# Two head pairs' queries and keys transposed on TensorE instead of by DMA, with a new written order of the whole kernel

## The chip, the cores and the metric

The kernel runs on one core of a Trainium2 chip. Its time is the device time of that core in microseconds (us), the median of several runs; the profile is that of one further execution. The engines are TensorE (PE, matrix products; PEld are its weight loads), VectorE (DVE), ScalarE (ACT), GpSimd (POOL) and SyncE (SP, which here only issues DMAs). Each engine works through its own instructions in order and waits where another engine or a DMA has not yet delivered.

## The reference, cut to what matters

A block-sparse attention is followed by a two-layer MLP with squared ReLU.

```python
B, H, S, D = 4, 8, 768, 64          # batches, heads, sequence, head size
scores = q @ k.T / sqrt(D)          # per batch and head, 768 x 768
mask = near the diagonal (blocks of 32, one to each side)
       | first or last block row or column
       | 3 sampled blocks of keys for each block of queries
attn = softmax(where(mask, scores, -1e9)) @ v
x = attn as 3072 tokens x 512
h = x @ w_in                        # 512 -> 2048
g = maximum(h, 0) ** 2
y = g @ w_out                       # 2048 -> 512
```

## The kernel before

**Tiling.** Two heads make a head pair (2 x 64 = 128 partitions), so there are 16 pairs, numbered u = 0 to 15; pair u belongs to batch u // 4. Queries come in three pieces of 256 columns. The scores are computed transposed (keys on the partitions), exponentiated by ACT (`exps`, line 360, and `s_exps`, line 643), masked, multiplied with the values (`values_full`, line 398, and `s_values`, line 673), normalized, transposed back (`x_transp`), and go as tiles of 256 tokens into the MLP: `hidden` (x with w_in), `relu` (lines 727 and 729), `square` (lines 738 and 740), and `out` matmuls with `out_copy` and `store`. Batches 0 and 1 compute all scores and mask them; batches 2 and 3 compute only the chosen blocks, with gathered keys and values. Nearly all matmuls are issued by one helper, `pair` (line 203), so the profile shows them as L203; copies and casts by `copy` (line 121 on ACT, 123 on DVE and POOL).

**PSUM.** Four cells of 1024 fp32 columns, called X, take the results of PE; a task names the cell that it uses.

**Queries and keys.** They arrive in fp32, are cast to bf16 (`cast_qk`, into a buffer `qc`) and must be transposed so that the head dimension is on the partitions (`QKT`). `prepare` builds the tasks for this. For the first four pairs, the transposes run on PE (`transp`, line 305) into an X cell, from which `evac` copies them to `QKT`. For pairs 4 and up a DMA transposes from `qc` to `QKT` directly (`transp_dma`, line 312), issued on SP's queue. `old_s` are the scores of the pair that used the same place of `QKT` before.

**The mask of the first two batches.** `mask_rows` (line 258) computes rows of the mask on PE, in two pieces (columns 0 to 256 and 256 to 768), and `mask_rows_evac` copies them to the bf16 tile `R2` (shown as R). In the first scores the mask is added on PE itself (matmuls `X<-R,oh`); the later masks are tiles made by `mask_tile` and `mask_evac` and are multiplied on DVE.

**Weights.** `w_load` (lines 328 and 331) loads w_in (0 to 3) and w_out (4 to 7) in eight parts of 512 KB on POOL's queue, starting once the last values of batch 0 have landed. `loads_gate` (line 338) puts two tiny DMAs into SP's queue that read from parts 6 and 7, so that the loads of batch 1 behind them (`load`, lines 149 and 151) start only when these two parts are there.

**The order.** The work is a list of tasks, and one long string, `PROGRAM`, says which task is issued when and on which engine. A word such as `P260/3` means: task 260 on PE, with cell 3 of PSUM; V, A, G and S stand for DVE, ACT, POOL and SP. `run_program` goes through the string once and issues the instructions; on each engine they then run in that order. Which engine does a cast, a square or a copy is chosen by the letter too.

```python
for word in PROGRAM.split():
    i, _, spot = word[1:].partition("/")
    t = tasks[int(i)]
```

Of the kernel before, what the change touches and what calls it, by code (L numbers as in the profile page):

```python
# [25 lines left out]
def kernel(  # L26
# [127 lines left out]
    KEYS, ALL = (slice(0, CP), slice(CP, NCH)), slice(0, NCH)  # L154
# [41 lines left out]
    X = [ps_x.tile([P, 1024], F32, name=f"X{i}").rearrange("p (h c) -> p h c", h=2) for i in range(NX)]  # L196
# [606 lines left out]
    def T_(f, *args, **kw):  # L803
        return Task((lambda e: f(*args, e)), **kw)
# [10 lines left out]

    def prepare(u):
        ev[u] = {}
        n_old = u - NPB
        old_s = sc_of[n_old] if n_old >= 0 else []
        old_v = va_of[n_old] if n_old >= 0 else []  # L820
        if u >= HP:
            g = gate[GATES[min(u - HP, len(GATES) - 1)]]
            for w in range(3):
                raw_of[u, w] = Buf(RAWS[w])
            ld_t = [T_(load, u, w, get=[raw_of[u, w]], deps=[g] + raw_claims[-1:]) for w in range(3)]
            at = [ld_t[2]]
            for w in (1, 0):
                qc = Buf("qc")
                c = T_(cast_qk, u, w, ALL, get=[qc], put=[raw_of[u, w]], deps=[ld_t[w]])
                buf_of["qc", u, w, 0] = qc  # L830
                cq[u, w] = [c]
                x = T_(transp_dma, u, w, deps=[c] + old_s, put=[qc])
                ev[u].update({(w, n): x for n in range(NCH)})
        else:
            at = []
            own = range(3 if u < 2 else 1 if u == 2 else 0)
            for w in own:
                raw_of[u, w] = Buf(RAWS[w])
# [116 lines left out]
    t = T_(table_load, deps=[])  # L955
# [3 lines left out]
    hb = Buf("X")  # L959
    t = T_(table_spread, hb, deps=[tb["slots"]], get=[hb], put=tmp)  # L960
# [3 lines left out]
    for us in [range(b * HP, (b + 1) * HP) for b in range(B)]:  # L964
        for u in us:
            prepare(u)
        mine = [a for a in order if a[0] in us]
        if us[0] < HP:
            for c0, c1 in MASKED:
                for n in range(0, NCH, 2):  # L970
                    mb = Buf("X")
                    t = T_(mask_tile, n, c0, c1, mb, get=[mb], deps=mr)
                    x = T_(mask_evac, n, c0, c1, deps=[t, mk_claims[[m_[0] for m_ in MASKED].index(c0)]], put=[mb])
                    for c in range(c0, c1, P):
                        mk[n, c] = mk[n + 1, c] = x
        if us[0] >= SB * HP:
            b = us[0] // HP
            vw = T_(v_store, b, deps=sum((cv[u] for u in us), []))
            for v in range(len(VISITS)):
                visit(b, v, vw, [a for a in mine if a[1] == v * P])  # L980
            continue
        for a in mine:
            attend(a, us[0] < HP and a[1] == 0)

    sq_of, gbuf = {}, {}
    for T in TILES:
# [3 lines left out]
        for f in range(0, NF, n_u):  # L990
            hb, ht, rb, gb = Buf("X"), Buf("H"), Buf("r"), Buf("g")
# [16 lines left out]
        for i, y in enumerate(ys):  # L1008
# [44 lines left out]
```

## Time and profile before

| | |
|---|---|
| median of 3 runs | 258.85 us (258.25 to 259.73) |
| the profiled execution | 258.04 us |
| its span in the trace | 256.3 us |
| PE busy | 244.4 us, 95% of the span, 5265 matmuls |
| ACT busy | 183.4 us, 72% |
| DVE busy | 173.0 us, 67% |
| POOL busy | 100.3 us, 39% |
| moved by DMA | 47.08 MB, 184 GB/s on average |

A profile has a page for the whole span (busy times, the chain of work that ended last, groups of instructions by line), and the trace behind it gives the single instructions. In a timeline row the columns are the start in us, the duration in us, the engine, the line of the code, the operation and its tiles as out<-in with their shapes, and in brackets the time that the engine had been idle before and what ended that. In a row of stretches there is for each engine the busy time and the number of its instructions, then PE's granted clock as a share of full speed, the busy share of the DMA engines and GB/s. In a row of groups, the busy sum and the mean duration in ns stand behind the first bar, the idle time before and its releasers behind the second. A row of the chain has start, length and what the chain was in.

### The profile page before, as it was taken

Reading aid. Unit: us, or ns where it says so; the run is one execution under the profiler, and the core shown is the slowest. Engines: PE = TensorE matmul, PEld = TensorE weight load, DVE = VectorE, ACT = ScalarE, POOL = GpSimd, SP = SyncE. Lnnn points to the kernel's source line nnn. Section 1 sums busy time; section 2 is a strip of 40 time slices with the busy share of each in tenths; the row PEclk is TensorE's granted clock in tenths of the full one; section 3 lists DMA queues with packets and bytes.
Section 4 is the critical chain, followed back from the end, with each engine's and each line's share of the span. In section 5 each row is a group of like instructions: output and inputs, shape, how many; then the busy total and the mean of one; then the engine's idle time right before and its main releaser. Section 6 shows DMA issues by size and latency. Waiting matters only on the chain.

```text
span 256.3 us, 12057 instructions
## 1 busy us (share of the span) xinstructions
PE 244.4 (95%) x5265; PEld 183.4 (72%) x5265; DVE 173.0 (67%) x411; ACT 183.4 (72%) x217; POOL 100.3 (39%) x178
## 2 busy tenths in 40 slices
PE   7988999989999999998999999999999999999994
PEld 5667779759975579975866766857774677666674
DVE  7678997789998999869939647656636725730301
ACT  3799999978999799946695975585965186623640
POOL 3264228002407006198558424174448620413100
PEclk9999999999999999999999999999999999999999
DMA  6999998999799997999589899996484922034122
GB/s 191 364 246 205 206 208 128 252 255 241 190 262 232 207 239 141 313 217 201 191 232 207 226 170 212 251 190 186 115 203 98 195 47 50 16 102 145 46 84 84
DMA packets 64692, 47.08 MB, mean 184 GB/s; under 512 B 31567, under 2 KB 60624, under 8 KB 64640
## 3 DMA queue, kind: packets, MB, share of 16 engines
q1 hardware_dynamic: 58512, 37.82, 63.0%
q0 software_dynamic: 5440, 8.05, 16.9%
q8 instruction: 41, 0.67, 1.2%
q10 hardware_dynamic: 688, 0.46, 0.6%
q14 instruction: 11, 0.09, 0.2%
HBM read 35.51 MB, written 7.91 MB: 169 GB/s over the span
## 4 chain that ended last, share of the span: by engine, by line
PE 68%; DMA 16%; DVE 4%; POOL 4%; SPq 3%; issue 2%; ACT 1%; DVEq 0%; POOLq 0%
PE X L203 63%; DMA w_out_sb<-in_moe_w_out_dram 5%; PE X L673 5%; DMA ys<-in_v_dram 3%; DMA QKT<-qc 3%; DMA ks<-in_k_dram 2%; DMA qs<-in_q_dram 2%; DMA VG<-rows 1%; SPq L556 1%; POOL qc L123 1%; POOL w_in_sb L328 1%; SPq L560 1%; POOL VB L123 1%; ACT pT L643 1%; POOL g L740 1%
## 5 line engine op out<-in xcount | busy, mean ns | idle before, releaser
L203 PE MATMUL X<-xT,w_in_sb 64*128 64x256 bf16 x1536 | 100.0, 269 | 0.6 <-issue 0.4
L203 PE MATMUL X<-w_out_sb,g 64*128 64x512 bf16 (+3 forms) x960 | 95.4, 334 | 0.2
L203 PEld LDWEIGHTS <-w_in_sb 64*128 64x128 bf16 x1536 | 74.9, 94 | 12.3 <-issue 1.2
L360 ACT ACTIVATE pT<-X 128x1024 bf16<-128x1024 f32 x72 | 70.4, 1031 | 8.5 <-PE X L203 8.0
L203 PEld LDWEIGHTS <-g 64*128 64x128 bf16 x960 | 40.2, 94 | 26.7 <-issue 0.6
L643 ACT ACTIVATE pT<-X 128x768 bf16<-128x768 f32 (+1 forms) x56 | 41.5, 765 | 24.2 <-PE X L203 20.9
L740 POOL TENSOR_TENSOR g<-r 128x1024 bf16<-128x1024 f32 (+1 forms) x20 | 31.6, 1587 | 67.3 <-ACT r L727 50.0
L727 ACT ACTIVATE r<-X 128x1024 f32<-128x1024 f32 x28 | 29.8, 1070 | 20.6 <-PE X L203 16.9
L729 DVE TENSOR_SCALAR r<-X 128x1024 f32<-128x1024 f32 x20 | 24.5, 1224 | 26.9 <-POOL g L740 10.2
L367 DVE TENSOR_TENSOR pT<-pT,VG 128x1024 bf16<-128x1024 bf16 x60 | 41.5, 724 | 0.7 <-ACT pT L360 0.7
L738 ACT ACTIVATE g<-r 128x1024 bf16<-128x1024 f32 (+1 forms) x40 | 35.3, 901 | 2.7 <-DVE r L729 2.5
L203 PE MATMUL X<-QKT 64*128 64x256 bf16 (+1 forms) x384 | 32.9, 255 | 3.8 <-DMA QKT<-qc 1.2
L650 DVE TENSOR_TENSOR pT<-pT,MKS 128x768 bf16<-128x768 bf16 (+1 forms) x48 | 28.6, 629 | 8.7 <-ACT pT L643 8.6
L203 PEld LDWEIGHTS <-QKT 64*128 64x128 bf16 x384 | 16.9, 97 | 10.5 <-issue 4.4
L597 POOL DMA_INDIRECT VG<-rows,idx x19 | 21.2, 1118 | 4.6 <-issue 2.3
L203 PEld LDWEIGHTS <-pT 64*128 64x128 bf16 x768 | 16.1, 94 | 2.3 <-issue 0.3
L203 PE MATMUL X<-VB,pT 64*128 64x65 bf16 x768 | 17.4, 190 | 0.2 <-issue 0.2
L203 PEld LDWEIGHTS <-KG 64*128 64x128 bf16 x528 | 13.7, 95 | 5.0 <-issue 0.7
L203 PE MATMUL X<-QKT,KG 64*128 64x64 bf16 x528 | 15.3, 190 | 0.3 <-issue 0.2
L673 PEld LDWEIGHTS <-pT 128*64 128x64 bf16 x624 | 11.9, 111 | 5.0 <-issue 3.3
L679 DVE RECIPROCAL ss<-X 128x8 f32<-128x8 f32 x12 | 2.5, 206 | 18.8 <-PE X L673 16.8
L121 ACT COPY ys<-X 128x1024 f32<-128x1024 f32 (+1 forms) x10 | 9.7, 970 | 6.5 <-PE X L203 4.2
(107 smaller groups left out, 211.8 us busy)
## 6 DMA issues: line engine op xcount, KB each, us to landing
vs<-in_v_dram SPq DMA_DIRECT2D x14, 384.0 KB
ks<-in_k_dram SPq DMA_DIRECT2D x13, 384.0 KB
qs<-in_q_dram SPq DMA_DIRECT2D x12, 384.0 KB
out_dram<-ys SPq DMA_DIRECT2D x9, 512.0 KB
VG<-rows SPq DMA_DIRECT2D x20, 132.0 KB
w_in_sb<-in_moe_w_in_dram POOLq DMA_DIRECT2D x4, 512.0 KB, 8.8
w_out_sb<-in_moe_w_out_dram POOLq DMA_DIRECT2D x4, 512.0 KB, 9.5
rows<-VB SPq DMA_DIRECT2D x2, 792.0 KB
```

What stands on the lines that cost most here:

```text
L121: A.copy(out=out, in_=in_)
L203: last = nc.tensor.matmul(out(r ^ crossed), lhsT(r ^ crossed, rows), rhs(r ^ crossed, rows), skip_group_check=True, **kw)
L360: A.activation(out=pT[:, :, 0:n], in_=stile.pop(a)[:, :, 0:n], func=AF.Exp, scale=scale)
L367: V.tensor_tensor(out=pT, in0=pT, in1=m[:, None].broadcast_to([P, 2, len(cs), w]), op=AOP.mult)
L597: G.indirect_dma_start(out=to[0:RS * HB], out_offset=None, in_=pairs, in_offset=bass.IndirectOffsetOnAxis(ap=idx[0:RS * HB, g - 1:g], axis=0))
L643: A.activation(out=pT[:, :, 0:n], in_=stile.pop((u, v, gs))[:, :, 0:n], func=AF.Exp, scale=scale)
L650: V.tensor_tensor(out=pT, in0=pT, in1=m[:, None].broadcast_to([P, 2, n]), op=AOP.mult)
L673: nc.tensor.matmul(po[i * D:(i + 1) * D, h, a * VW:(a + 1) * VW], pts[g][:, h, c * D:(c + 1) * D], val, start=a == 0 and c == 0, stop=c == ...
L727: A.activation(out=to, in_=src, func=AF.Relu)
L729: V.tensor_scalar(out=to, in0=src, scalar1=0.0, scalar2=None, op0=AOP.max)
L738: A.activation(out=g, in_=r, func=AF.Square)
L740: (G if e == "POOL" else V).tensor_mul(out=g, in0=r, in1=r)
```

## The change

For pairs 4 and 5, the first two pairs of the second batch, queries and keys are transposed on PE into an X cell and copied to `QKT`, as for the first four pairs, in place of the DMA transpose: 48 transposes and four copies for four DMAs. The other pairs keep the DMA. Behind that, the string `PROGRAM` is new as a whole; the numbers of the tasks behind pair 4 shift by up to four.

```diff
+    BY_PE = (4,5)
+
     def prepare(u):
         ...
                 c = T_(cast_qk, u, w, ALL, get=[qc], put=[raw_of[u, w]], deps=[ld_t[w]])
                 buf_of["qc", u, w, 0] = qc
                 cq[u, w] = [c]
-                x = T_(transp_dma, u, w, deps=[c] + old_s, put=[qc])
+                if u in BY_PE:
+                    hb = Buf("X")
+                    t = T_(transp, u, w, ALL, hb, deps=[c], get=[hb], put=[qc])
+                    x = T_(evac, u, w, ALL, deps=[t] + old_s, put=[hb])
+                else:
+                    x = T_(transp_dma, u, w, deps=[c] + old_s, put=[qc])
                 ev[u].update({(w, n): x for n in range(NCH)})
...
-    PROGRAM = """A29 G35 P4/3 V32 P30/0 P12/2 P14/3 P9/1 P5/1 V31 P33/1 V111 P36/3 P0/2 A37 V1 V34 P102/2 ...
+    PROGRAM = """
+        S21 P2/0 S18 P0/3 A29 G35 P4/1 V1 V3 V32 P30/3 P12/2 P14/1 P9/2 P5/1 V31 P33/2 V111 P36/1 A37 V34 P102/0 V209 V46 P47/3 P106/2
...
```

What the new order moves, by engine:

- The start: the two `mask_rows` (P2 and P0) stand first on PE, and their copies (V1, V3) first on DVE, ahead of the cast of the second half of pair 0's keys (V32). Before, P0 stood behind the first transposes and P2 behind the scores of pair 1.
- The load of the table of sampled blocks (S21) stands first in SP's queue; POOL works out the table's places ahead of the weight loads.
- The weight loads on POOL's queue come in the order 1, 2, 7, 0, 6, 3, 4, 5 (before: 1, 2, 0, 3, 7, 6, 4, 5). POOL's casts of the values of pair 1 (G52) and pair 3 (G73) stand behind three and seven of them (before: behind two and three).
- Behind the gate SP issues the loads of keys 5, queries 4, queries 5, keys 4, values 4, queries 6. The casts are on POOL (queries 4, queries 5), DVE (keys 4) and ACT (keys 5), and the copies of the transposes on DVE (pair 4) and ACT (pair 5).
- All eight output parts of the first MLP tile stand ahead of the first scores of pair 4 on PE (before: four of them).
- Squares: ACT 24 (before 40), POOL 18 (20), DVE 18 (0). ReLUs: ACT 32 (28), DVE 16 (20). Casts of queries and keys: ACT 5 (2), POOL 22 (14), DVE 10 (21). Casts of values: ACT 2 (0), POOL 9 (10), DVE 5 (6). Output copies: ACT 7 (11), DVE 8 (4).
- The last piece of the output is 256 columns wide (before: 128).

More of the change, by code (lines that the diff above doesn't have):

```diff
@@ new lines @@
+    PROGRAM = """
+        S21 P2/0 S18 P0/3 A29 G35 P4/1 V1 V3 V32 P30/3 P12/2 P14/1 P9/2 P5/1 V31 P33/2 V111 P36/1 A37 V34 P102/0 V209 V46 P47/3 P106/2
+        A103 V48 P104/1 V43 A107 P44/3 G57 P7/0 V45 A105 P58/0 V54 P113/3 V59 P55/1 A114 P117/0 G41 V56 V67 A118 P115/1 P108/0 A116 V64
+        P127/3 V109 P10/2 P65/1 A128 P123/2 V66 A124 P68/1 P125/3 G22 G75 V69 V63 P92/1 P110 A126 P133/2 G76 G81 G38 G49 V112 A134 P39/0
+        P137/3 G52 S83 S19 S28 S20 S42 V40 V93 P88/0 A60 A138 V155 V89 P84/2 P119/1 G74 V70 V85 P61/3 P86/0 P135/2 V62 V120 G80 G77 G78
+        G73 A87 A136 P129/3 P121 V130 V122 P176/0 P131 P170/1 P139/2 A177 A171 V132 V140 P50/0 P71/3 P146/1 P141 V72 V142 V51 A147
+        P149/3 V172 A150 P173/2 V148 P785/0 A174 P786 V178 P189/1 P787 A190 V175 P90/3 P15/2 P96/2 P788 V91 P143/1 P8/3 A97 P183/2 V151
+        A789 P94/3 P179/0 V95 A184 G79 G791 P16/3 P186/2 P11/3 P778/3 V180 P779 A144 A790 V145 V191 P181 P157/1 P780 V185 V182 A187
+        P163/2 P781 V188 A158 A782 P152/0 P217/1 P792/3 A164 P793 P160/2 P794 P795 A218 A161 A796 P799/1 V159 V153 V300 V165 V162 V219
+        P800 P154 P192/2 V193 P166/3 A156 P100/0 P194 P801 P802 V167 V195 S82 S53 S264 S253 S263 S254 A783 A784 A101 S255 S273 P168
+        P214/0 P211/2 A215 G798 G797 G259 V169 P822/3 V803 P823 P828/0 P824 P196/1 A212 P825 V216 V826 V213 V256 A266 A197 P829 P199/2
+        A200 P830 P831 P202/1 P260/3 G805 G804 P816/2 G269 P817 P818 A203 P257/1 P819 V261 V258 A832 G278 A262 A820 P806/3 P228/1 P220/0
+        S274 S275 P807 S281 S442 S282 S279 S466 S283 P231/2 S338 A229 A276 P221 P245/1 P808 V827 V833 V222 V198 P223 P809 A246 A232
+        P239/1 A240 V224 V204 V201 P810 P267/2 P270/0 P811 P242/1 A271 P205/0 P812 A268 A286 A243 P206 P225/2 P813 V247 V230 V280 V821
+        V233 V241 V207 G284 G288 G447 P292/1 A226 S277 S443 P208 P834/2 P835 S285 S265 S287 S451 A293 P295/1 A210 A296 V814 V227 V244
+        P836 P98/0 P837 P234/3 P302/1 P235 G272 G445 V99 A838 P248/0 V236 P289/2 P249 P237 V250 V294 A303 A238 P308/3 P305/1 P251 A290
+        A252 A309 P317/2 P850/0 V291 V304 V297 P851 P856/3 P852 A306 A318 P853 A854 P857 P298/1 P320/2 P299 A855 P858 A321 V839 P868/0
+        V310 V307 V301 V319 V322 S444 P859 P869 P314/1 P870 S450 S459 S460 P359/2 P871 S446 S448 S458 S440 A860 P840/3 P841 G449 G453
+        A315 A861 A360 V872 P311/1 P329/0 P312 P326/2 V313 V316 P842 P862/1 A327 P863 P353/2 A330 P843 P332/0 A354 A333 P864 P323/2 P865
+        A866 V331 V328 V361 V334 P324 P844 P335/0 V325 V355 P356/1 P336 P343/2 P845 A465 A357 P346/1 P846 A344 P847 A347 V337 V358
+        P340/0 P362/2 P365/1 P363 A848 A341 P874/3 P875 G873 G455 P368/0 G471 G461 G867 P876 A366 P877 P377/1 S468 S454 S467 S456 S339
+        S627 S626 S815 S452 S472 S462 A369 A378 V351 V23 V345 V348 V342 P371/0 P878 V364 A372 P879 P349/1 P380/0 P350 P383/2 A381 P880
+        P407/0 V373 V367 V352 V370 P881 P404/1 V382 V379 A384 A408 P374/2 G473 G469 G463 G631 G629 P890/0 P375 A405 A882 P891 P397/1
+        P892 V385 V376 P391/3 P386/2 A398 A392 P387 P410/1 V457 V406 V388 P893 V409 V399 P431/3 P394/2 A411 A395 A432 P24/1 P884/2 P885
+        S470 S849 S618 S389 S390 S474 S620 S475 S612 S611 S619 S883 S464 S477 P896/3 V402 V412 V396 V27 V26 P886 V25 A894 P434/0 P897
+        P887 P898 P899 A435 A888 P413/0 P419/1 P414 G895 G889 A900 P428/2 P930/3 P931 A420 P932 P902/1 P903 P933 P904 V393 V421 V415
+        V478 V436 P905 A901 A429 P400/2 P908/0 P401 A934 V403 V433 V430 P422/3 G507 A906 P918/1 P919 P416/2 A935 A423 A417 P920 P909
+        G613 G476 P936/3 P921 P437/2 P937 P438 V424 V418 G625 V508 A922 A907 P938 P939 V439 P425/1 P910 P486/2 P426 P911 V617 V427 A940
+        A487 P489/3 P491/2 P496/1 P912 A941 A492 A497 P484/2 P479/1 A480 A485 P913 V488 V923 V498 V493 S635 S632 P914 P494/1 P915 P481/2
+        S441 S634 S628 S503 A490 A495 P924/3 P925 A482 V916 V483 P515/2 P926 G505 G550 G637 S630 S614 S506 S544 S546 P927 P499/1 G639
+        S524 S549 S501 P952/0 A928 G504 G525 V500 V551 P953 P958/3 P954 P509/1 A516 A929 A510 P955 P959 P518/2 P512/1 P960 G528 G526
+        G548 A519 V956 V957 P961 P561/2 P942/0 A513 A562 A962 P943 P555/1 P552/2 P944 V621 V633 V517 V520 V511 V529 V514 P945 P558/3
+        P946 A553 A556 P964/1 A963 A559 P965 P521/2 P947 P539/3 P948 P949 V554 V563 V522 G547 G593 P533/2 A540 P966 A534 P970/3 P971
+        V557 V560 V594 P967 V950 V541 P972 P973 P530/0 P976/2 S610 S502 S636 A974 P977 V968 P564/1 G641 G623 S638 S622 S589 S527 A969
+        A531 S523 S567 P978 P536/3 P598/0 V535 V975 V565 V532 G590 G569 G591 G571 G568 P979 A537 P601/1 P992/3 V615 V538 P993 A599 A602
+        P998/0 P994 P999 P995 P542/1 P980 P1000 P1001 V543 V603 V572 V1002 V600 P604/1 S917 S616 S642 A996 S566 P1004/3 S545 S712 S592
+        S951 S587 S624 S643 P1005 A997 A605 P981 P576/1 P986/0 P1006 A577 P987 P579/1 P1007 P988 A580 P989 A1008 V606 V581 V990 P595/1
+        P982 P582/3 P983 G1003 A596 P1038/0 P573/1 G1009 G644 A583 P1039 A574 P1026/3 P1040 P1027 P647/1 V597 V584 V984 A991 P1041 P1028
+        P607/2 A1042 V608 V646 V578 P1032/0 P1029 P1033 P1010/2 P1034 A648 A1030 P1035 V1036 V575 P1011 P652/1 S570 P659/3 P1012 P6/0
+        P585/0 S671 S645 S669 S692 S640 S672 S609 S985 V1043 A1031 A653 A660 P654/1 P1013 A655 V586 V661 P649/3 P657/1 P1014 G673 G675
+        A658 A650 P1020/0 P1015 P664/3 P1021 P662/1 P1016 P1017 A665 A663 V656 V651 V666 V676 P667/3 P677/1 P1022 V668 S588 S735 S695
+        S738 S674 A1018 G696 G1037 G693 P683/2 P1023 P1054/3 A678 P680/1 P1055 A684 P1066/2 P1056 P1067 A1024 A681 P686/0 V697 P1057
+        V1025 P1068 V679 V1058 P1069 P704/1 G736 G737 G718 G694 A687 P1044/0 P1072/3 A705 P1045 P701/1 P1073 A702 V688 V1059 P1046 P13/1
+        P1047 V685 V1070 P698/2 P1060/1 P1074 P1075 P1061 V703 V682 V1071 V719 A699 P689/2 A1076 P1048 P723/3 A1077 A724 P1062 V690 V700
+        P1063 V725 V1064 V706 P720/2 P1049 P729/3 P1050 P1051 P707/1 A730 A721 A1065 A708 P726/3 S670 S714 P1078/2 S691 G739 G715 G761
+        P1079 V731 V722 V709 V740 P1094/1 A1052 A727 P1095 P710/0 P1088/3 P1096 P1097 P1080 P1081 P1089 V728 V1098 S757 S716 S717 S759
+        S755 P1100/1 P1101 P1090 V711 P1091 P1102 P732/0 S1053 S713 S1019 V733 P1082 A1099 P1103 V762 A1092 P744/3 V1093 V1104 V1105
+        P1106/0 A745 P1107 P1083 P769/3 S734 G758 S760 A770 P1084 P1108 P747/1 P766/3 P1109 P1085 A748 A1110 P1143/1 P1144 P750/0 V746
+        V1086 P1145 A767 P772/3 P1146 A751 A773 V1147 P763/2 P1122/0 P1123 G1149 P741/3 P1124 P1125 P1112/1 A764 A1111 A1126 A742
+        P1136/2 V774 V752 V1148 V749 V771 V768 P1137 P1113 V743 V765 G1128 P1114 P1138 P753/0 P1129/3 P1130 V754 P1139 P775/0 P1131
+        G1127 P1115 P1132 V776 P1116 S756 S777 P1117 P1118 P1150/0 P1119 A1140 A1133 A1120 G1135 G1134 P1151 P1167/2 P1168 P17/3 V1141
+        V1142 P1160/1 P1174/3 P1169 P1175 P1152 P1170 P1161 P1176 P1162 P1153 S1121 S1087 P1163 P1177 A1171 A1172 A1173 P1181/2 P1182
+        V1164 A1165 A1178 P1154 P1183 P1184 P1155 V1179 G1166 P1156 P1208/1 P1209 V1185 V1186 P1157 P1218/3 V1158 A1180 A1187 P1219
+        P1188/2 P1189 P1210 P1211 P1190 P1212 P1191 P1220 P1221 P1192 P1222 P1193 P1198/0 P1194 P1223 P1213 P1195 P1214 P1215 P1199
+        P1200 P1224 P1201 A1196 P1225 P1202 V1216 A1226 S1159 P1203 S1197 P1204 P1205 V1206 S1217 S1227 S1207
@@ L1022 @@
+    """
     run_program({"y": 99, "S": 99, "H": 99, "po": 99, "pT": PT_BUFS, "r": R_BUFS, "g": G_BUFS, "ys": YS_BUFS, "qc": QC_BUFS, "xq": XQ_BUFS, "xT": XT_BUFS, "vg": VG_BUFS, "kg": KG_BUFS, "xs": 2, "qs": NRAW, "ks": NRAW - 1, "vs": NRAW - 1})
```

1 line of the change is left out of this document (removed).

## The prediction

> **What bounds the kernel now.** I read the page first (totals, then the chain of work that ended last), then the busy time by stretch of the span, and then the timeline at the places where TensorE (PE) has gaps.
>
> ```profile
> span 256.3 us, 12057 instructions
> PE 244.4 (95%) x5265; PEld 183.4 (72%) x5265; DVE 173.0 (67%) x411; ACT 183.4 (72%) x217; POOL 100.3 (39%) x178
> ...
> PE 68%; DMA 16%; DVE 4%; POOL 4%; SPq 3%; issue 2%; ACT 1%; DVEq 0%; POOLq 0%
> ```
>
> PE is the bound: busy for 95% of the span and 68% of the chain. What is not PE in the chain is mostly DMA, and it belongs to the first 55 us. The table by stretch says where PE is not full.
>
> ```profile
> core 0: us, PE busy (x) PEld busy (x) DVE busy (x) ACT busy (x) POOL busy (x), PEclk, DMA share, GB/s
> 0.00:25.00 25.00, 20.87 (x382) 15.61 (x384) 18.16 (x52) 18.21 (x21) 11.02 (x26) 1.00 0.98 253
> 25.00:50.00 25.00, 24.81 (x516) 20.57 (x514) 21.27 (x39) 24.66 (x32) 9.21 (x17) 1.00 1.08 200
> 50.00:55.00 5.00, 3.80 (x99) 2.36 (x93) 4.97 (x12) 3.52 (x4) 0.00 (x0) 1.00 1.18 205
> 55.00:115.00 60.00, 59.46 (x1387) 47.42 (x1385) 52.62 (x127) 52.81 (x58) 20.32 (x31) 1.00 1.00 231
> 115.00:125.00 10.00, 9.10 (x212) 6.19 (x210) 9.97 (x27) 5.83 (x8) 8.06 (x15) 1.00 0.84 157
> 125.00:190.00 65.00, 64.24 (x1419) 47.29 (x1416) 40.82 (x113) 47.66 (x59) 33.05 (x64) 1.00 0.93 204
> 190.00:205.00 15.00, 14.33 (x288) 9.11 (x284) 9.40 (x23) 5.62 (x8) 9.47 (x19) 1.00 0.69 158
> 205.00:250.00 45.00, 44.94 (x854) 32.25 (x850) 15.06 (x24) 24.81 (x32) 9.15 (x7) 1.00 0.25 70
> 250.00:256.30 6.30, 2.81 (x156) 2.57 (x150) 0.72 (x2) 0.27 (x1) 0.00 (x0) 1.00 0.25 86
> ```
>
> PE stands idle 4.1 us in the first 25 us and 3.5 us behind 250. Between 25 and 250 it is idle for only 0.19 + 1.20 + 0.54 + 0.90 + 0.76 + 0.67 + 0.06 = 4.32 us. So a better order behind the start can win about 4 us at the very most by taking waits away, while any wait that it adds on PE is paid in full. Beside PE, ACT is nearly as full from 10 to 50 us, with under 2 us of slack:
>
> ```profile
> 10.00:50.00 40.00, 37.76 (x793) 30.60 (x795) 33.31 (x69) 38.07 (x47) 17.34 (x29) 1.00 1.09 222
> ```
>
> **The start: mask rows first.** On PE both mask-row matmuls now stand ahead of the first transposes, and on DVE both of their copies (256 and 512 columns) ahead of the cast of the second half of the first keys. The timeline of before:
>
> ```profile
> 4.16 0.18 DVE L249 TENSOR_SCALAR bm<-r 24x48 bf16<-24x48 f32 x1
> ...
> 4.50 0.55 DVE L123 CAST qc<-ks 128x384 bf16<-128x384 f32 x1 [0.17 <-DMA ks<-in_k_dram]
> ...
> 5.37 0.40 PE L258 MATMUL X<-oh,bm 64*128 64x256 bf16 x1
> 5.60 0.37 ACT L121 COPY QKT<-X 128x256 bf16<-128x256 bf16 x1 [1.66 <-PE X L305]
> ...
> 5.81 0.42 DVE L123 CAST R<-X 128x256 bf16<-128x256 f32 x1 [0.49 <-PE X L258]
> ...
> 6.29 0.40 PE L203 MATMUL X<-QKT 64*128 64x256 bf16 x2 [0.52 <-DVE R L123]
> ...
> 8.50 0.42 PE L203 MATMUL X<-QKT 64*128 64x256 bf16 x2
> ...
> 11.12 0.35 PE L305 MATMUL X<-identb,qc 64*128 64x64 bf16 x12 [0.16 <-DVE qc L123]
> 11.31 0.27 PE L203 MATMUL X<-QKT 64*128 64x256 bf16 x2
> ...
> 11.74 0.38 PE L258 MATMUL X<-oh,bm 64*128 64x512 bf16 x1
> ...
> 12.19 0.68 DVE L123 CAST R<-X 128x512 bf16<-128x512 f32 x1
> ```
>
> The first scores now wait for the copy of the 256 mask columns, which ends at 6.23. In the new order the mask operand is ready at 4.34, as before; the second matmul starts some 0.4 later at 4.77, and its copy 0.44 behind that (5.81 less 5.37) at 5.21, to 5.63. Then comes the 512 copy, 0.68, to 6.31, and only then the cast of the keys, 0.55, to 6.86, which ended at 5.05 before. From that cast to the end of the queries' copy before it took 5.97 - 5.05 = 0.92; so the first scores start near 7.8 in place of 6.29, +1.5. What comes back is the matmul and the copy at 11.74 and 12.19, which stand between scores there: 0.38 on PE. Bounds: 0 (ACT's exponentials set the pace soon after and the delay is made up) to +1.5; I take +1.1, since ACT has no slack to make it up in.
>
> **Weight loads and the casts of values on POOL.** Seven of the eight weight loads now stand in bundles of three and four, and the value casts of head pairs 1 and 3 behind more of them.
>
> ```profile
> 14.90 1.76 POOL L328 DMA_DIRECT2D w_in_sb<-in_moe_w_in_dram  x2
> 16.64 0.86 POOL L123 CAST VB<-vs 128x768 bf16<-128x768 f32 x1
> ...
> 17.96 0.77 POOL L328 DMA_DIRECT2D w_in_sb<-in_moe_w_in_dram  x1
> ```
> ```profile
> 17.99 0.91 PE L398 MATMUL X<-VB,pT 128*128 128x65 bf16 x24
> ```
>
> Ahead of the cast at 16.64 come one more load (0.77) and two casts of queries that followed it before (I price them at 0.65 each, three quarters of the value cast's 0.86, an estimate): it ends near 17.50 + 0.77 + 1.3 = 19.5, and its matmuls ran at 17.99. With the start 1.1 later they are due at 19.1. The cast of pair 3 stands behind four more loads. Bounds 0 to +1.5 (19.5 - 17.99); I take +0.5. The table load moved to the front of SP's queue and the table's places to POOL's idle time before 14.90 cost nothing: PE asks for neither before 65 us. If the gate of the weights passes earlier, the next loads start earlier, which counts below.
>
> **48 transposes on PE for four on the DMA queue.** Twelve transposes took 0.35 at full clock (11.12), so four groups take 1.4, and PE has no gap to hold them; upper bound 2.1 at the half clock seen at 8.50. I take +1.4. The four copies from PSUM (two on ACT, two on DVE) are 128x768 each; a 512-column cast from PSUM took 0.68, so each is under 1 us, off PE's path as long as the scores come later: zero here, up to +1 if ACT hands its lateness on. What goes is this chain of before:
>
> ```profile
> 35.20 4.66 DMA ks<-in_k_dram
> 40.01 0.82 POOL qc L123
> ...
> 44.60 8.11 DMA QKT<-qc
> ```
> ```profile
> 50.62 1.03 PE L203 MATMUL X<-w_out_sb,g 64*128 64x512 bf16 x8
> 52.85 0.40 PE L203 MATMUL X<-QKT 64*128 64x256 bf16 x4 [1.20 <-DMA QKT<-qc]
> ```
>
> A DMA transpose landed 8.11 behind its issue, and PE waited 1.20 for it. By PE and a copy the same tile is there about 1.4 after its cast, so this wait goes: -1.2, with 0 as the other end if what is late next (below) is as late. The order also puts all eight output parts of the first MLP tile ahead of the first scores of pair 4, four more than before at 1.03 each, so these scores come near 58 and need the batch later; the other pairs of that batch (6 and 7) keep the DMA transpose and have the shorter queue.
>
> **What is late next: the loads.** A transpose on PE stands in PE's queue: if its cast is not done, all of PE waits, which a DMA did not make it do. Four loads of 384 KB (keys 5, queries 4 and 5, keys 4) stand together behind the gate, and the cast of keys 4 on DVE and of keys 5 on ACT, in front of exponentials, come some 14 us of PE work ahead of the first scores of pair 4 (an estimate, by the instructions that the order has between them and the page's mean durations): near 45. At the 200 GB/s of that stretch four loads take 7.9 us, from 35.2 to 43.1: in time by 2 us. If the last two weight loads (512 KB each, 5.2 us at that rate) share the queues it is 48.3, and 3.3 late. Bounds 0 to +3.3; I take +0.5.
>
> **The place at 119 us.** The order between 115 and 125 is wholly new.
>
> ```profile
> 119.33 0.29 PE L203 MATMUL X<-xT,w_in_sb 64*128 64x256 bf16 x2 [0.40 <-issue]
> 120.08 0.37 PE L203 MATMUL X<-QKT 64*128 64x64 bf16 x12 [0.45 <-ACT g L738]
> 120.27 2.32 PE L203 MATMUL X<-w_out_sb,g 64*128 64x512 bf16 x16
> ```
>
> Gaps of 0.40 and 0.45 and 0.26 of slow running (2.32 against twice 1.03) are 1.1 us that this order lost here, in a stretch where DVE is busy 9.97 of 10. I take -0.7 of the 0 to -1.1: the place is new, but what else is moved fills DVE.
>
> ```profile
> L729 DVE TENSOR_SCALAR r<-X 128x1024 f32<-128x1024 f32 x20 | 24.5, 1224 | 26.9 <-POOL g L740 10.2
> ```
>
> Eighteen squares go from ACT (16) and POOL (2) to DVE, where none is in the trace; by this nearest row they cost DVE up to 22 us. Eleven casts of queries and keys (0.55 each) and four of these relus leave it: 11 us more on 173. Its cover is that it is busy for 67% only; where it is full, each square is a possible wait of 1.2 for the output matmuls, which the range holds. The shape of the last pieces changes (the last is 256 columns wide, was 128): behind 250 us PE's 2.81 of 6.30 says that the end is copies and stores; zero, up to +0.5.
>
> **The sum:** 1.1 + 0.5 + 1.4 - 1.2 + 0.5 - 0.7 = +1.6 us. Against the profiled execution's 258.04 that is 259.6. That execution lies 0.8 below the median of the three runs, 258.85, and the changed kernel is measured by its own median, so I add the sum to the median: about 260.5, 0.6% slower. A difference under 0.5% (1.3 us) can't be told from no change here; so 257.6 to 260.1 is the same, and the forecast stands just outside, with its own range of 258.9 (both delays of the start made up) to 261.8.
>
> **Rivals.** *Fewer waits behind the start (faster).* Half of what PE loses is waits that an order could avoid. For it: the middle is new everywhere, and ACT, the fullest beside PE up to 50 us, gives work away. Against it: only 4.32 us of idle time are there, and DVE, which takes the squares, is full at 115 to 125. Price: the start's terms made up (0), transposes +1.4, waits at 52 and 119 gone (-2.3), and all but 0.3 of the other 2.2 us of idle time: -2.8, so 256.0. It decides if the first scores of pair 4 find everything ready and PE's idle time from 25 to 250 is under 1 us.
>
> *The loads come late and PE stands behind a cast.* For it: the row of 200 GB/s with a DMA share of 1.08 and the two weight loads that may run beside them. Against it: the 2 us in hand. Price: 3.3 in place of 0.5, so 260.5 + 2.8 = 263.3. The same time results if ACT waits for a later load in front of exponentials.
>
> *The clock of PE rises later.* Two matmuls took 0.42 at 8.50 and 0.27 at 11.31: PE runs at half speed until about 10.5, 4.2 us after the first scores. In the new order PE has only 14 short instructions between the mask rows and scores near 7.8. If that gap costs a further stretch of 4.2 us at half speed, the work in it takes 2.1 more: 262.6. The Trainium skill ("TensorE: Matmul & The Clock Gate", Part 1: The HAM clock gate) says that the gate opens after about 3.4 us of sustained activity, counted in a window that runs freely and doesn't start with the kernel. The trace has the two speeds and a rise of that order (4.2 us), though PE had been active on warm-up matmuls for longer; by the rule the time of the rise could even stay at 10.5 when the scores start later, and the sum would then lose some 0.7 of its start term (259.8). I hold to the rows and let the rise move with the scores.
>
> *The transposes by DMA were hidden but for chance (the change does little).* If the wait at 52.85 is taken over by the exponentials, since ACT is 38.07 of 40 busy, nothing is won for the 1.4 of transposes: 260.5 + 1.2 = 261.7.
>
> **Chances.** The forecast with its own range 0.39, of which 0.23 falls within 0.5% and 0.16 above; fewer waits 0.33 (0.32 of it over 0.5% faster); late loads 0.15; a late clock 0.07; nothing won 0.06. So faster 0.32, same 0.24, slower 0.44. The range runs from 255.0 (the faster rival with another microsecond) to 264.3 (late loads with the end's 0.5 and the upper price of the transposes), with about one in ten outside at each end.
>
> **What would show it.** The first scores near 7.8 with DVE's key cast as the releaser; values of pair 1 waiting for POOL near 19; no wait on QKT by DMA for pair 4; 48 more transposes, of 0.35 for twelve; PE idle between 25 and 250 near 3 us. The prediction is wrong if that idle time is under 1 us (faster), if a transpose of pairs 4 or 5 waits on a cast for over 2 us, or if matmuls still take 0.42 behind 12 us.

## The result and the profile after

The changed kernel takes 270.04 us (267.74 to 272.25, 4 runs), the kernel before 258.55 us beside it: a ratio of 1.041, 95% interval 1.031 to 1.051. By the medians it is 11.5 us slower, where the forecast was 1.6 us slower and the range ended at 264.3. The ratios here and below leave out executions that took over 1.5% longer than the fastest of the same kernel, so a ratio can be smaller than that of the two medians. On another chip and in a third run the ratio was the same (1.040 and 1.039), while the time before was 254.7 and 258.5; so runs are compared by ratios to the kernel before on the same chip.

The page of the changed kernel's profile (span, busy times, chain):

```profile
span 266.9 us, 12134 instructions
PE 248.7 (93%) x5313; PEld 183.4 (69%) x5313; DVE 186.1 (70%) x411; ACT 177.9 (67%) x209; POOL 108.4 (41%) x190
...
PE 83%; DVE 7%; ACT 7%; issue 2%; ACTq 0%; DVEq 0%
```

DMA, 16% of the chain before, is gone from it, and DVE and ACT took its place with 14% (5% before): the transposes on PE did what they were to do. But PE also waits more. Its busy time by three stretches, first of the changed kernel, then of the kernel before (columns as in the table of the prediction):

```profile
0.00:25.00 25.00, 20.15 (x334) 14.49 (x335) 15.79 (x46) 15.99 (x19) 14.05 (x37) 1.00 1.00 260
25.00:250.00 225.00, 214.96 (x4649) 158.19 (x4647) 164.68 (x358) 157.68 (x185) 93.36 (x152) 1.00 0.76 172
250.00:266.90 16.90, 13.61 (x340) 10.72 (x334) 5.68 (x7) 4.20 (x7) 1.04 (x1) 0.97 0.18 65
```
```profile
25.00:250.00 225.00, 220.68 (x4739) 165.19 (x4737) 154.10 (x358) 164.91 (x196) 89.26 (x152) 1.00 0.82 179
```

Of the 10.6 us between the spans, 0.7 are idle time of PE before 25 us (4.85 against 4.13), 5.7 are idle time from 25 to 250 (10.04 against 4.32; all of it lies behind 55, where PE was busy 192.07 of 195 us before and 186.22 now), 0.2 come back behind 250, and 4.4 are busy time (248.72 against 244.36). The group of transposes explains 1.2 of that last part (5.2 us busy for 144, 4.0 for 96 before). By the lengths of its matmuls PE went from half to full speed near 13.2 us in place of 10.6, which makes up about 1.3 more (an estimate: 2.6 us at half speed). The rest, about 1.9, is matmuls that take longer on the record, and I did not split it.

No single wait makes up the 5.7: the longest two behind 55 us are 1.28 and 1.13 us, and the others are under 0.7. These two can be read off the timeline of the changed kernel, at about 60 and 230 us:

```profile
57.63 1.21 DVE L740 TENSOR_TENSOR g<-r 128x1024 bf16<-128x1024 f32 x1
58.77 1.91 DVE L367 TENSOR_TENSOR pT<-pT,VG 128x1024 bf16<-128x1024 bf16 x2
58.96 1.18 POOL L123 CAST VB<-vs 128x768 bf16<-128x768 f32 x1 [1.66 <-DMA vs<-in_v_dram]
...
60.80 0.42 DVE L413 TENSOR_TENSOR xq<-X,rs 128x256 bf16<-128x256 f32 x1
61.28 0.23 PE L427 MATMUL X<-identb,xq 64*128 64x64 bf16 x4 [1.13 <-DVE xq L413]
```
```profile
229.90 2.54 POOL L740 TENSOR_TENSOR g<-r 128x512 bf16<-128x512 f32 x2 [0.69 <-ACT r L727]
230.15 4.11 DVE L650 TENSOR_TENSOR pT<-pT,MKS 128x768 bf16<-128x768 bf16 x5
233.85 0.95 PE L673 MATMUL X<-VG,pT 128*64 128x65 bf16 x48 [1.28 <-DVE pT L650]
```

In both PE waits for DVE, 1.13 us for a normalized tile behind a square and two masks, and 1.28 us for masks; and in both POOL works beside DVE's masks. Masks take longer on the whole; the larger of their two groups, first in the changed kernel, then before:

```profile
L367 DVE TENSOR_TENSOR pT<-pT,VG 128x1024 bf16<-128x1024 bf16 x60 | 45.1, 793 | 5.2 <-ACT pT L360 2.8 <-issue 2.3
```
```profile
L367 DVE TENSOR_TENSOR pT<-pT,VG 128x1024 bf16<-128x1024 bf16 x60 | 41.5, 724 | 0.7 <-ACT pT L360 0.7
```

In the other group (line 650) the 40 masks of 128x768 take 699 ns on the mean, 638 before.

Near 142 and 149 `s_values` (matmuls with gathered values) take 1.5 us more than their usual 0.95 in one profile of the changed kernel and 3.7 in another. One of these gaps ends with gathered values that land; for the others the profile names no releaser, so that late gathers are behind all of them is likely, not shown.

### The profile page after: what moved, and what is told of

Read it like the earlier page. It is cut to its first block, busy times and chain, and to the rows that moved or that the text cites. A ratio compares the mean times of both kernels' runs of the same rounds, so it can differ in the third digit from the quotient of the medians.

```text
span 266.9 us, 12134 instructions
## 1 busy us (share of the span) xinstructions
PE 248.7 (93%) x5313; PEld 183.4 (69%) x5313; DVE 186.1 (70%) x411; ACT 177.9 (67%) x209; POOL 108.4 (41%) x190
## 4 chain that ended last, share of the span: by engine, by line
PE 83%; DVE 7%; ACT 7%; issue 2%; ACTq 0%; DVEq 0%
PE X L203 75%; PE X L673 5%; ACT pT L360 4%; DVE pT L650 2%; PE X L398 2%; ACT pT L643 1%; PE X L305 1%; DVE pT L367 1%; DVE QKT L123 1%; DVE VG L279 1%; DVE xq L413 0%; DVE qc L123 0%; DVE r L729 0%; ACT QKT L121 0%; DVE R L123 0%
## 5 line engine op out<-in xcount | busy, mean ns | idle before, releaser
L203 PE MATMUL X<-w_out_sb,g 64*128 64x512 bf16 (+3 forms) x960 | 94.1, 334 | 0.0
L740 POOL TENSOR_TENSOR g<-r 128x512 bf16<-128x512 f32 (+1 forms) x18 | 26.5, 1482 | 66.8 <-DVE r L729 36.5
L367 DVE TENSOR_TENSOR pT<-pT,VG 128x1024 bf16<-128x1024 bf16 x60 | 45.1, 793 | 5.2 <-ACT pT L360 2.8
L727 ACT ACTIVATE r<-X 128x1024 f32<-128x1024 f32 x32 | 33.7, 1060 | 22.6 <-PE X L203 22.4
L650 DVE TENSOR_TENSOR pT<-pT,MKS 128x768 bf16<-128x768 bf16 (+1 forms) x48 | 30.5, 662 | 5.9 <-ACT pT L643 5.7
L729 DVE TENSOR_SCALAR r<-X 128x1024 f32<-128x1024 f32 x16 | 19.5, 1218 | 16.9 <-PE X L203 16.9
L738 ACT ACTIVATE g<-r 128x1024 bf16<-128x1024 f32 (+1 forms) x24 | 21.9, 922 | 7.1 <-DVE r L729 6.9
L740 DVE TENSOR_TENSOR g<-r 128x1024 bf16<-128x1024 f32 (+1 forms) x18 | 19.4, 1086 | 3.6 <-ACT r L727 3.4
L123 POOL CAST qc<-qs 128x384 bf16<-128x384 f32 (+3 forms) x21 | 13.4, 656 | 17.1 <-DMA QKT<-qc 11.4
L612 POOL COPY KG<-QKT 128x256 int32<-128x256 int32 x10 | 6.2, 616 | 27.5 <-PE X L203 27.4
```

The source lines that it names most:

```text
L123: (V if e == "DVE" else G).tensor_copy(out=out, in_=in_)
L203: last = nc.tensor.matmul(out(r ^ crossed), lhsT(r ^ crossed, rows), rhs(r ^ crossed, rows), skip_group_check=True, **kw)
L367: V.tensor_tensor(out=pT, in0=pT, in1=m[:, None].broadcast_to([P, 2, len(cs), w]), op=AOP.mult)
L650: V.tensor_tensor(out=pT, in0=pT, in1=m[:, None].broadcast_to([P, 2, n]), op=AOP.mult)
L727: A.activation(out=to, in_=src, func=AF.Relu)
L729: V.tensor_scalar(out=to, in0=src, scalar1=0.0, scalar2=None, op0=AOP.max)
```

## The experiments

The theory after the result (A): the time is lost in many waits that the new written order makes on engines that work in order, most of them behind 55 us. Rivals: (B) the transposes on PE cost it; (C) the late start throws everything behind it out of step; (A1) it is the new choice of engines (squares on DVE), not the sequence; its counterpart (A2) is that the sequence makes the waits and is matched to its own engines.

### The transposes alone, in the old order

```diff
 ... P223 
+P257/1 P260/2 V258 V261          (pair 4: transposes, copies on DVE)
 ... P292/0 ... P810
+P270/1 P267/0 A271 A268          (pair 5: transposes, copies on ACT)
-S257 S259 S265 S267 of before    (DMA transposes)
```

> The order of before, with only the eight tasks exchanged: queries and keys of pairs 4 and 5 are transposed on PE and copied (pair 4 on DVE, pair 5 on ACT), each right behind a place where its cast was done in the trace of before. Theory A (the new order costs the time, in many waits of its own; the transposes are cheap): 258.55 + 1.4 for the transposes - 1.2 for the wait at 52.85 + 0 to 1.5 for two copies on a full DVE, so 258 to 260.5. Theory B (the transposes on PE cost it, because PE stands behind casts and cells of PSUM): 264 or more.

Measured: 260.15 us beside 254.39, a ratio of 1.021 (1.016 to 1.025): 5.3 us by the ratio, not 0 to 2. In the timeline PE waits for a cell that a copy on ACT holds; this is a quarter of the loss, and the rest is not traced to a wait:

```profile
54.55 0.23 PE L203 MATMUL X<-warm 64*128 64x128 bf16 x2 [1.28 <-ACT QKT L121]
```

So the same transposes were placed with all copies on DVE, pair 5's directly behind the first scores of pair 4:

```diff
-A271 A268
+P270/1 V271 P267/1 V268     (directly behind P292)
```

> The old order with the 48 transposes on PE again, but all four copies on DVE and the transposes of pair 5 directly behind the first scores of pair 4. In the first such run PE waited 1.28 for a PSUM cell that a copy on ACT, behind an exponential and a square, let go late. If that wait was the cost: a ratio of 1.00 to 1.008 instead of 1.021. If any insertion into the old order costs this much, since everything behind it shifts: 1.015 to 1.025.

Measured: 1.017 (1.010 to 1.023). The wait for ACT is gone and one for DVE is there instead (0.72 us at 53.79). Even only the twelve transposes for the one DMA that PE waited for bring no gain:

```diff
-S259                        (DMA transpose of the queries of pair 4)
+P259/1 ... V260             (12 transposes, one copy on DVE)
```

> The old order with only the queries of pair 4 on PE: 12 transposes and one copy on DVE for the one DMA transpose whose landing (8.11 us) made PE wait 1.20 at 52.85. Sum: 0.35 - 1.2 = -0.85, a ratio of 0.996 to 1.00, if the gain is kept; 1.005 or more if the order behind it loses what was won.

Measured: 1.004 (1.000 to 1.008). PE now waits 1.19 us for that copy on DVE, as long as it had waited for the DMA:

```profile
49.74 0.40 PE L203 MATMUL X<-QKT 64*128 64x256 bf16 x4 [1.19 <-DVE QKT L123]
```

So in the old order the 48 transposes on PE are a loss by themselves, of about half the change's 4%; for twelve of them no difference can be told. This is more than theory A allowed and less than theory B.

### The new order without them

```diff
-    BY_PE = (4,5)
+    BY_PE = ()
-P257 P260 P267 P270 and V258 V261 A268 A271
+S257 S259 S265 S267         (each directly behind its cast)
```

> The order of the changed kernel, with the transposes of pairs 4 and 5 by DMA again, each issued right behind its cast. Theory A: the new waits stay; 270 - 1.4 for the transposes + 0 to 1.5 for a DMA that lands late, so 268 to 271. Theory B: 264 or less, near the kernel before.

Measured: 273.48 us, 1.060 (1.051 to 1.070), slower than the changed kernel, which was at 1.040 on the same chip. In the new order, with the DMA transposes placed as here, the transposes on PE are a gain of about 2%. The four DMA transposes hold SP's queue from 43.40 to 52.86 us, 4.2 of it behind the first one, until a cast of keys on DVE ends at 48.95, and about 1.2 for the issue of each. The load of keys behind them is issued at 52.91, where the changed kernel issues it at 45.57; ACT stands 5.14 us at a cast of keys whose load has not landed, the exponentials behind it come late, and PE stands still for 4.43 us and then runs at half clock. The profiled execution took 275.76 us, the longest of four (the shortest 268.06), so how much of the 1.060 this gap makes up isn't shown. In the rows of stretches the last columns are PE's granted clock, the DMA share and GB/s:

```profile
57.05 0.83 ACT L121 CAST qc<-ks 128x768 bf16<-128x768 f32 x1 [5.14 <-DMA ks<-in_k_dram]
57.79 2.85 ACT L360 ACTIVATE pT<-X 128x1024 bf16<-128x1024 f32 x3
...
58.86 0.61 PE L203 MATMUL X<-QKT 64*128 64x256 bf16 x4 [4.43 <-ACT pT L360]
```
```profile
54.00:56.00 2.00, 0.43 (x4) 0.09 (x1) 1.11 (x2) 0.00 (x0) 0.00 (x0) 1.00 0.92 138
56.00:58.00 2.00, 0.00 (x0) 0.00 (x0) 0.00 (x0) 0.95 (x2) 0.00 (x0) 0.90 1.05 369
58.00:60.00 2.00, 1.14 (x8) 0.66 (x9) 1.16 (x2) 2.00 (x3) 0.00 (x0) 0.50 1.10 311
60.00:62.00 2.00, 2.00 (x12) 0.88 (x10) 2.00 (x4) 1.35 (x2) 0.00 (x0) 0.50 1.16 276
62.00:64.00 2.00, 2.00 (x35) 1.37 (x32) 1.57 (x2) 0.66 (x1) 0.97 (x1) 0.50 1.15 302
64.00:66.00 2.00, 2.00 (x42) 1.25 (x40) 0.45 (x2) 0.58 (x2) 0.92 (x2) 0.90 1.17 320
```

Theory B falls for the new order: it is as slow without the transposes on PE.

### The start alone

```diff
-... P33/1 V111 P36/3 P0/2 A37 V1 ... P2/1 ... V3     (the order of before)
+P2/1 P0/2 A29 G35 P4/3 V1 V3 V32 ...
```

> The kernel before (transposes by DMA), with nothing changed but the two mask-row matmuls and their copies, moved to the front as in the changed kernel. First scores near 7.7 instead of 6.29. The start term of the prediction by itself: +1.1 us (0 to +1.5), a ratio of 1.004. If the old order is thrown out of step by any delay: 1.015 or more.

Measured: 1.0038 (1.0004 to 1.0071), which is 1.0 us. The order behind is not thrown out of step by it. In this profile PE doesn't wait for a DMA transpose of queries or keys, although every DMA is as before: the scores of pair 4, at 52.85 before, start at 51.93 with no idle time before them.

### Stage by stage

Three kernels take the first words from one order and the rest from the other; all have the transposes on PE.

```diff
 PROGRAM = first 156 words (to about 27 us) of the old order + the rest of the new     (first)
 PROGRAM = first 365 words (to about 65 us) of the old order + the rest of the new     (second)
 PROGRAM = first 156 words (to about 29 us) of the new order + the rest of the old     (third)
```

> Transposes on PE; the first 156 words of the order (to about 27 us) as in before, the rest in the new order. By the two traces PE had lost 2.3 us more by then than before. If lost time at the start is simply handed on (theory A): 270 - 2 to 3.5, so 266.5 to 268. If the late start is what throws everything behind it out of step (theory C): 262 or less.

Measured: 1.039 (1.031 to 1.046), beside 1.040 for the changed kernel on the same chip; no gain from the old start can be seen, and the intervals leave room for one of under 1%.

> Transposes on PE; the first 365 words (to about 65 us) in the old order, the rest in the new one. By the two traces 4.8 us of the loss lie before this point. Theory A (each stretch has waits of its own): 258.5 to 260 for the first part and some 5 us more for the rest, 263 to 266. Theory C (only the first part is bad and the rest suffers by it): 259 to 261.

Measured: 1.084 (1.078 to 1.089), far outside both theories. PE has two gaps at and behind the seam, 4.80 us at 75.50 for a normalized tile and 4.61 us at 161.71 for a transposing DMA, each with a stretch at half clock behind it.

> The first 156 words (to about 29 us) in the new order, with the mask rows first, the rest in the old order with the transposes on PE. The old order with transposes on PE was at 1.021. If the start's lost time is handed on: 1.021 + 2.3 us/258 = 1.03. If it is made up: 1.02. If a late start throws the old order out of step: 1.04 or more.

Measured: 1.043 (1.035 to 1.052), with 4.0 us of waiting for the DMA transpose of x. By the first, theory C in its simple form falls: it asked for 262 us or less beside 258.55, a ratio of 1.013. By the second and the third, theory A in the form of losses that add up by stretch falls as well. The third came out where its expectation had put a late start that throws the old order out of step; but the mask rows alone didn't do that (1.004), and whether it is the rest of the new start or the seam is open. In these runs a part of an order can't be priced by itself.

### Engines or sequence

```diff
 the order of words as in the changed kernel, 86 letters as before, such as
-V821 (square)   A838 (ReLU)   A266 (cast of keys 5)
+A821            V838          V266
```

> The new order of words, but the 86 tasks that changed their engine (squares, ReLUs, casts, a few copies) are on the engine of before. Theory A1 (the squares and copies on DVE make the masks late, and PE waits for masks): a ratio of 1.01 to 1.025. Theory A2 (the sequence itself makes the waits, and is matched to its own engines): 1.035 to 1.06.

Measured: 291.65 us, 1.148 (1.139 to 1.157), over three times the loss of the change itself.

> The order of before with DMA transposes, but the same 86 tasks on the engine that the changed kernel gives them. Theory A1: a ratio of 1.015 to 1.03. Theory A2: 1.00 to 1.015, or, if any order suffers when its engines are changed, as much as in the run beside it.

Measured: 1.054 (1.047 to 1.062). A1 falls by the first run: with the engines of before the new sequence is not better but far worse. The second came out above the bounds of both theories: the new engines in the old sequence cost more than the whole change. So each sequence fits its own engines (A2), though A2's bounds were too narrow. The longest single waits of PE in the first run are for a normalized tile on DVE, 2.6 us, and for squares on ACT, 2.2.

### Mending single waits of the new order

The changed kernel itself was run again beside two groups of these.

> The changed kernel itself once more, so that the next three stand beside it on one chip. Before was 254.4 where the first four ran and 258.6 where the changed kernel ran, so ratios are compared: 1.04, by all theories.

Measured: 1.040 (1.033 to 1.046).

> The changed kernel once more, as the measure for the three beside it: 1.04.

Measured: 1.039 (1.033 to 1.045).

Two squares near 230 us to ACT:

```diff
-G1128 G1127
+A1128 A1127
```

> The changed kernel, with two squares near 230 us (the halves of the first hidden group of tile (3, 256)) on ACT instead of POOL. In both profiles of the changed kernel s_values of that place waits 1.28 us for DVE's masks, while POOL runs these squares and the masks take 1.4 us instead of 0.54. Theory P (POOL and DVE slow each other when they work at the same time): the masks there go back to 0.5 to 0.7 each, the wait of 1.28 is gone, and the ratio falls by 0.004 to 0.007, to about 1.034. Theory Q (the masks are late only because DVE has too much in front of them): masks still at 1.4, wait 1 us or more.

Measured: 1.033 (1.027 to 1.039). The rows at the place, now of this kernel:

```profile
229.76 2.42 DVE L650 TENSOR_TENSOR pT<-pT,MKS 128x768 bf16<-128x768 bf16 x5
229.99 1.16 ACT L738 ACTIVATE g<-r 128x512 bf16<-128x512 f32 x2
...
232.11 0.95 PE L673 MATMUL X<-VG,pT 128*64 128x65 bf16 x48
```

The same five masks take 2.42 us where they took 4.11 with POOL's squares beside them, in all three profiles of the changed kernel, and PE's wait of 1.28 is gone. The two masks just before, beside a POOL square that stayed, take 1.86 in both kernels. Theory P is right, by this wait; the ratios' intervals overlap, so the gain in time (about 0.7%) is likely but not certain. The Trainium skill ("SBUF — State Buffer", Who interferes with whom) says that a DVE instruction with two inputs in SBUF contends with a GpSimd instruction that reads SBUF, since they share a port pair; the trace agrees, 4.11 against 2.42.

Three tasks off ACT near 57 us:

```diff
-A271 A268 A286
+V271 V268 G286
```

> The changed kernel with three tasks taken off ACT near 57 us: both copies of pair 5's transposes go to DVE, the cast of pair 7's queries to POOL. In the profile of the changed kernel they hold up three exponentials, and PE waits there for a PSUM cell (1.3 and 0.7 us in its two profiles). If ACT's lateness is what PE pays (theory A): that wait gone, 0.7 to 1.3 us less, 0.003 to 0.005 off the ratio. If DVE is as full: no change or more.

Measured: 1.059 (1.055 to 1.064). The expectation had read the place wrongly: PE waited there less for ACT than for the normalization on DVE (the row at 61.28 above; 0.50, 1.13 and 1.44 us in the three profiles of the changed kernel). With the copies on DVE as well, that wait grows to 3.08. This is about 2 of the 5 us lost; the profile is of the shortest of six executions, and where the others lose more isn't shown:

```profile
63.58 0.23 PE L427 MATMUL X<-identb,xq 64*128 64x64 bf16 x4 [3.08 <-DVE xq L413]
```

Gathers of values ahead of a gather of keys on POOL:

```diff
-G528 G526 G548 ... G547
+G526 G548 G547 G528
```

> The changed kernel with three gathers of values (visits 2 and 3 of batch 2) moved ahead of one gather of keys on POOL's queue, which took 3.2 us there because DVE ran one at the same time. In the two profiles of the changed kernel s_values of visits 1 and 3 lose 1.5 and 3.7 us near 142 and 149, the one in one run and the other in the other, on gathered values that land late. If the late gathers are the part that differs from run to run: no such loss at s_values of visit 3, 1.5 to 3.5 us less, a ratio of 1.027 to 1.035 and a smaller spread. If the wait only moves to the next gathered tile: 1.04.

Measured: 1.058 (1.053 to 1.063). The values are there in time, but the keys that the gather G528 brings are late, and PE runs scores and hidden matmuls in pieces. (The expectation puts the 3.2 us of that gather down to another on DVE; by the trace of the changed kernel DVE ran a square, casts and masks beside it, from 135.58 to 138.79, and no gather.)

```profile
132.47 0.41 PE L203 MATMUL X<-xT,w_in_sb 64*128 64x256 bf16 x4 [0.26 <-issue]
133.19 0.38 PE L203 MATMUL X<-xT,w_in_sb 64*128 64x256 bf16 x3 [0.32 <-issue]
133.91 0.25 PE L203 MATMUL X<-QKT,KG 64*128 64x64 bf16 x5 [0.34 <-issue]
135.50 0.26 PE L203 MATMUL X<-QKT,KG 64*128 64x64 bf16 x3 [1.35 <-issue]
```

All four mends at once (the mask rows back in their old places too):

> The changed kernel with all four mends: mask rows back in the places of before, the three tasks off ACT, the gathers ahead, the two squares near 230 on ACT. If the waits are separate and add up: 1.0 + 1.0 + 2 + 1.4 = 5.4 us less, a ratio of 1.02. If a wait that is taken away mostly uncovers the next: 1.03 or more.

Measured: 1.061 (1.056 to 1.066). Matched matmul by matmul to the changed kernel on the same chip, it is 3.4 us ahead at 16 us, 3.1 behind at 65, 10.3 behind at 143 and 7.3 behind at 236: it wins the start and the end and loses near 20 (2.0 us for a cast on POOL), 60 and 135. About half of the early lead is not the mend: its clock was full from 5.2 us, and the run with the gathers moved, also full early, was 1.9 us ahead at 16 us with the mask rows where the changed kernel has them. Of the four mends two made things worse alone, one likely helped, and the mask rows weren't moved alone in the new order; the waits don't add.

## Why the prediction was wrong

The direction was forecast, the size was not: +1.6 forecast, +11.5 measured. The range's upper end adds up to 264.5, not 264.3, by its own terms (263.3 + 0.5 + 0.7), which changes nothing. By its steps:

- **The start, +1.1.** Right as a chain: the first scores start at 7.71 (7.8 forecast), and the same move alone in the old order costs 1.0 us. In the changed kernel's profile it cost more: the first matmuls with values start at 14.67, where they started at 12.67 before, as the clock rose later too (see the rivals). The chain is seen here:

```profile
4.40 0.82 PE L258 MATMUL X<-oh,bm 64*128 64x512 bf16 x2
5.26 1.02 DVE L123 CAST R<-X 128x256 bf16<-128x256 f32 x2 [0.91 <-PE X L258]
6.20 0.54 DVE L123 CAST qc<-ks 128x384 bf16<-128x384 f32 x1
...
7.71 0.40 PE L203 MATMUL X<-QKT 64*128 64x256 bf16 x2 [0.47 <-ACT QKT L121]
```

- **Casts of values on POOL, +0.5.** No PE wait for them in the changed kernel: zero, within the bounds. With the old start they were late by 1.42 us.
- **48 transposes, +1.4, and the DMA wait, -1.2.** Each was right as an item (0.35 for twelve; no wait for that DMA), but the sum of the two, near zero, was not: in the old order it was 4 to 5 us (1.017 and 1.021), in the new one a gain of about 2%. The copies from PSUM were priced at zero "as long as the scores come later", with up to +1; in the runs PE waited 1.28, 0.72 or 1.19 for exactly these copies and for cells that they held. And the wait of 1.20 was a matter of one profile: with the same DMAs and the mask rows first it didn't occur.
- **Loads ahead of PE's transposes, +0.5.** Zero; PE waited for no cast of a late load there (0.2 us for `qc` in all).
- **The place at 119, -0.7.** That gap is gone, but it was worth little beside the next point.
- **The step that failed** is the one behind the sentence that any wait which the new order adds on PE is paid in full. It was said and then not priced: the sum had no term for the order behind 55 us except the gains, although all of it was new. The traces showed +5.85 us of idle time there (8.78 against 2.93). What I had taken for a cover, that DVE is "busy for 67% only", was none: a mean over the span says nothing on what stands ahead of a mask or a normalization in DVE's queue at one moment. A square and masks slowed by POOL stand ahead of what PE waits for at 61 us, masks slowed by POOL at 233, and PE waited near 142, likely for late gathers.
- **Rivals.** The late clock did occur: matmuls still took 0.42 at 12.15, and 0.27 from 13.28 (before, 0.27 from 10.69); that had been named as a sign of it. It came as an addition, of about 1.3 us by the rival's own reckoning, and not as the whole. That the rise moves with the scores doesn't hold: of four profiles with the start of before, two matmuls of the scores take 0.42 until 8.76 or later in two, and 0.27 from the first scores at 6.0 to 6.3 in the two others. The rival of the late loads didn't occur in the changed kernel; its second form, ACT at a cast in front of exponentials, occurred word for word in the new order with DMA transposes. "Nothing won" was right in the old order and wrong in the new.

How much of the 11.5 us belongs to which wait behind 55 us stays open: the runs show that the parts don't add up, so such a split may not exist. That the new order loses as much without the transposes on PE is shown (1.060); which property of it does so is not, since other disturbed orders lost as much or more.

## What to carry to other kernels

When a written order of a kernel whose main engine is 95% busy is replaced as a whole, the price can lie in waits that no row of the old trace shows; put a term on it (here it was some 4%), and don't set it to zero because each single item is cheap. A wait in one profile isn't a gain to be had: ask what releases the engine next, which queue the replacement's work joins, and whether the wait is there in a second profile. Small patches to a balanced order seldom won here: of five (two or three engine letters, a few words moved, or one DMA replaced), two cost about 2%, two about 0.4% (one of these not told from nothing), and one likely won 0.7%.

## What the runs showed of the hardware

A gap of 4.4 us on PE halved its clock: in the run with DMA transposes in the new order the last matmul before the gap ended near 54.4, the granted clock fell to 0.50 near 57.6 and came back near 64.4, though PE worked from 58.86 on. So the gap cost its length and about 2.8 us more (an estimate: 5.5 us at half speed). The Trainium skill ("TensorE: Matmul & The Clock Gate", Part 1: The HAM clock gate) gives at least one window of some 3.4 us for both the fall and the rise; the fall agrees (3.2 us behind the last matmul), and the rise took more than one such length here (5.5).

This is a part of what made disturbed orders dear. Inside the kernels the stretches at half clock lasted 3.4 or 6.8 us, as from 74.8 to 78.2 and from 160.1 to 166.9 in the second splice. Each of PE's waits of 3.38 (all four mends, at 63.17), 4.02 (the third splice), 4.43, 4.61 and 4.80 us brought one; a wait of 3.08 (three tasks off ACT) did not. Shorter waits close together could do it as well: in the second profile of the changed kernel the clock fell at 153.0, behind waits of 0.87 and 2.36 us. With the gathers moved the clock fell at 135.1 behind waits of under 0.4 us each and one not yet over, PE having been busy for 1.50 us of the four from 132 to 136.

The first scores met either clock, with nothing in the kernels that differs so far: with the same start, in the changed kernel's third run and in the one with the gathers moved, the first scores took

```profile
7.94 0.40 PE L203 MATMUL X<-QKT 64*128 64x256 bf16 x2 [0.47 <-ACT QKT L121]
```
```profile
7.64 0.28 PE L203 MATMUL X<-QKT 64*128 64x256 bf16 x2 [0.47 <-ACT QKT L121]
```

and 8.5 us later the second was 1.9 us ahead. The old start shows the same, in four profiles of orders that don't differ up to there: the first matmuls with values start at 12.67 (before) and 12.46 where the first scores met the half clock, and at 10.77 and 10.98 where they met the full one. So two single profiles can differ by some 1.5 to 1.9 us by the clock that the start meets. In the run with the mask rows moved alone, PE started the scores at full clock (0.29 at 7.53), fell back to 0.46 at 8.49 and was at 0.27 again at 11.99. The prediction tied the rise to the first scores; it isn't tied to them. The Trainium skill ("TensorE: Matmul & The Clock Gate", Part 1: The HAM clock gate) would have it so, with a window that runs freely and doesn't start with the kernel.
